# A two-stage kernel (attention to inducing points, then a SwiGLU feed-forward): its 128x128 turns on TensorE are replaced by 32x32 block turns on VectorE

## The chip, the cores and the metric

The kernel runs on one core of a Trainium2 chip. The metric is the device time of one execution in microseconds (us), taken as the median of several runs. A trace of one further execution, taken by the hardware profiler, shows what each engine did: TensorE (PE; its weight loads are listed apart as PEld), VectorE (DVE), ScalarE (ACT), GpSimd (POOL) and SyncE (SP, which here only issues DMAs).

## The reference

Four batches of 12,416 tokens with 128 channels go through attention to 32 inducing points and back, and every token then goes through a feed-forward of width 1,536. All arithmetic is in float32; the three weights arrive as 64-bit floats.

```python
def mab(q, kv):
    s = scale * (q @ kv.transpose(0, 2, 1))
    s = s - s.max(-1, keepdims=True)
    a = np.exp(s); a /= a.sum(-1, keepdims=True) + 1e-09
    return a @ kv
h = mab(I, x)              # per batch: 32 inducing points attend to 12416 tokens
y = mab(x, h)              # the tokens attend to the 32 rows of h
rms = np.sqrt(np.mean(y * y, -1, keepdims=True) + 1e-06)
yn = y / rms * rms_g
g = yn @ w_gate            # 128 -> 1536
out = (g / (1 + np.exp(-g)) * (yn @ w_val)) @ w_out
```

## The kernel before

**The algebra.** A token's y is a mixture of the 32 rows of h. The kernel therefore never forms y for the feed-forward: once per batch it multiplies h (scaled by rms_g) into w_gate and w_val (`stack`, the tiles sg and sv), and feeds the FFN with the token's 32 mixture weights. The weights and the stacks are both split into a high and a low part in the format fp32r, so the contraction is 4 x 32 = 128 rows.

**The FFN.** A unit is 512 tokens (two units of a batch are shorter: 25 units per batch, 100 in all). For each unit, `ffn` runs 12 slots j. A slot is two fp32r matmuls (g, line 504, and v, line 506, into four PSUM banks "gv"), a Silu on ACT (line 508), a product on DVE (u, line 510, which reads v from PSUM) and a float32 matmul with w_out into the accumulator acc (`project`, line 487), which is delayed by two slots with the list `late`. Because four gv banks hold two slots, g of a slot waits for the Silu of two slots before, and v for the product u of two slots before. A finished acc is copied by ACT (oT, line 499), turned on PE by four 128x128 transposes (line 492), copied by DVE (line 494) and stored by one DMA in pieces of 2 KB.

**What is laid between the slots.** `slot(j)` puts other steps behind the g, v, Silu and u of a slot and ahead of its project. Two lists feed it. The attention of the next batch is spread evenly over the slots: turns of x on PE (`turn_x`, line 242, evacuated by DVE and ACT in turn, lines 215 and 217), scores (line 250), one exp of the whole batch on ACT (`exp1`, line 293), turns of the exponentials (line 308) and sums into h (line 320), second scores (line 366) and their turns (line 375), maximum and subtraction on DVE (lines 378 and 379), a second exp (line 383) and the stacks (line 392). The `seam` of the next set of four units runs at fixed slots (`plan`): turn the weights (line 423), form y only for its mean square (a matmul with a block diagonal of h, line 437, a Square on ACT, line 439, a sum on DVE, line 440), take the power -0.5 on POOL (line 447), scale the weights (line 449), turn them back (line 454) and split them into hi and lo (lines 458 and 459). The last step, `split`, has the place (2, 10): third unit of the set, slot 10. At slot 2 of each unit, `gather` copies the next unit's hi and lo rows into the moving tile a with four DMAs.

**The front.** Ahead of the first slot, batch 0's attention runs alone, and the nine pieces of the weights are loaded one by one, converted to float32 by eight DVE operations and one on POOL each, and w_gate and w_val are stored to DRAM for the later batches. Every DMA but two is issued by SP in program order, so a DMA that waits holds up those behind it.

Of the kernel before, what the change touches and what calls it, by code (L numbers as in the profile page):

```python
# [11 lines left out]
I32 = mybir.dt.int32  # L12
# [8 lines left out]
TB = 4  # L21
GB = R * TB


@with_exitstack
def kernel(
# [26 lines left out]

    nc = tc.nc
# [3 lines left out]
    NB = N // P  # L58
    NJ = F // P
    NG = NB // GB  # L60
    H = P // 2
    SCALE = float(1.0 / (C ** 0.5))
    assert C == P and m * R == P and F % 512 == 0 and N % P == 0
    assert NG >= 1 and NB - NG * GB in (0, 1)


    groups = [(g * GB, GB, R, TB) for g in range(NG)]
    if NB > NG * GB:
        groups.append((NG * GB, 1, 1, 1))
    tail = len(groups) > NG  # L70
    TAIL0 = NG * TB * P
    SCW = max(TAIL0 + (P if tail else 0), NB * m)

    sizes = [TB] * (NB // TB) + ([NB % TB] if NB % TB else [])
    if sizes[-1] == 1:
        sizes[-2:] = [TB - 1, 2]
    units = [(sum(sizes[:u]), n) for u, n in enumerate(sizes)]
    NU = len(units)  # L80
    sets = [list(range(s, min(s + R, NU))) for s in range(0, NU, R)]

    def chunks(s):

        at = 0
        for t in range(TB):
            rows = m * sum(units[u][1] > t for u in sets[s])
            if rows:
                yield t, rows, at
            at += rows  # L90

    def rects(s):

        found = []
        for q, u in enumerate(sets[s]):
            n = units[u][1] * P
            if found and found[-1][2] == n:
                found[-1][1] = (q + 1) * m
            else:
                found.append([q * m, (q + 1) * m, n])  # L100
        return found

    def first(s):
        return units[sets[s][0]][0]

    def count(s):
        return sum(units[u][1] for u in sets[s])
# [5 lines left out]
    xnp = pool("xnp", NG)  # L113
    scp = pool("scp", 2)
    stk = pool("stk", 2)
    small = pool("small", 2)
    work = pool("work", 3)
# [4 lines left out]
    up = pool("up", 4)  # L122
# [5 lines left out]
    xT = const.tile([P, NB * P], F32, name="xT")  # L128
    xnat = {}
    xv = x.rearrange("b (p j) c -> b p j c", j=NB)  # L130
    ov = out.rearrange("(b p j) c -> b p j c", b=B, j=NB)

    def load_x(b, g):
        j0, nb, nq, nt = groups[g]
        tag = "xn" if g < NG else "xnt"
        t = xnat[b, g] = xnp.tile([P, nb, C], F32, name=tag, tag=tag, bufs=NG if g < NG else 1)
        nc.sync.dma_start(out=t[:], in_=xv[b, :, j0:j0 + nb, :])

    load_x(0, 0)
# [4 lines left out]
    for g in range(1, len(groups)):  # L144
        load_x(0, g)
# [3 lines left out]
    w32 = [[dram.tile([P, 512], F32, name=f"w{i}{c}") for c in range(F // 512)] for i in range(2)]  # L149
# [4 lines left out]
    mhalf = const.tile([P, GB], F32, name="mhalf")  # L154
# [13 lines left out]
    raws = []  # L168

    def load_w(i, c):  # L170

        src, k = (moe_w_gate, moe_w_val, moe_w_out)[i], 512 // C
        dst = work.tile([P, 512], F32, name="w", tag="sq") if i < 2 else wo.rearrange("p j c -> p (j c)")[:, ts(c, 512)]
        load_w32(i, c, src, dst[:] if i < 2 else dst, k)
        if i < 2:  # L180
            nc.sync.dma_start(out=w32[i][c][:], in_=dst[:])

    def load_w32(i, c, src, dst, k):
        src = src[:, ts(c, 512)] if i < 2 else src[ts(c, k * P), :].rearrange("(j p) c -> p j c", p=P)
        if src.dtype == F32:
            nc.sync.dma_start(out=dst if i < 2 else dst.rearrange("p (j c) -> p j c", c=C), in_=src)
            return
        if not raws:
            t = scp.tile([P, SCW], F32, name="sc")
            raws.extend(t[:, ts(n, 1024)] for n in range(SCW // 1024))  # L190
        words = raws.pop(0).bitcast(I32)
        nc.sync.dma_start(out=words if i < 2 else words.rearrange("p (j c) -> p j c", j=k), in_=src.bitcast(I32))
        raw = words.rearrange("p (f w) -> p f w", w=2)
        low, high = raw[:, :, 0], raw[:, :, 1]
        e, s = (up.tile([P, 512], I32, name="u") for _ in range(2))
        f, r = (silp.tile([P, 512], F32, name="silu") for _ in range(2))
        fi = f.bitcast(I32)
        ve = nc.vector
        ve.tensor_scalar(out=e[:], in0=high, scalar1=20, scalar2=0x7FF, op0=ALU.logical_shift_right, op1=ALU.bitwise_and)
        ve.tensor_scalar(out=e[:], in0=e[:], scalar1=896.0, scalar2=1151.0, op0=ALU.max, op1=ALU.min)  # L200
        ve.tensor_scalar(out=e[:], in0=e[:], scalar1=-896.0, scalar2=float(1 << 23), op0=ALU.add, op1=ALU.mult)
        ve.tensor_scalar(out=s[:], in0=high, scalar1=-(1 << 31), scalar2=0x3F800000, op0=ALU.bitwise_and, op1=ALU.bitwise_or)
        ve.tensor_scalar(out=fi[:], in0=high, scalar1=12, scalar2=9, op0=ALU.logical_shift_left, op1=ALU.logical_shift_right)
        ve.tensor_tensor(out=fi[:], in0=fi[:], in1=s[:], op=ALU.bitwise_or)
        ve.scalar_tensor_tensor(out=r[:], in0=low.bitcast(U32), scalar=2.0 ** -52, in1=s.bitcast(F32)[:],
                                op0=ALU.mult, op1=ALU.mult)
        ve.tensor_tensor(out=f[:], in0=f[:], in1=r[:], op=ALU.add)
        nc.gpsimd.tensor_tensor(out=dst, in0=f[:], in1=e.bitcast(F32)[:], op=ALU.mult)

    turn = [0]  # L210

    def evacuate(dst, src):
        turn[0] += 1
        if turn[0] % 2:
            nc.vector.tensor_copy(out=dst, in_=src)  # L215
        else:
            nc.scalar.copy(out=dst, in_=src)  # L217

    sc, diag, stacks = {}, {}, {}

    def attention(b, load_next):

        st = {}
        steps = []
        add = steps.append

        def open_():
            sc[b] = scp.tile([P, SCW], F32, name="sc")
            st["gmx"] = small.tile([P, len(groups)], F32, name="gmx")

        add(open_)
# [6 lines left out]
        def turn_x(g, q):  # L238
            j0, nb, nq, nt = groups[g]
            ps = bank()  # L240
            for t in range(nt):
                nc.tensor.transpose(ps[:, ts(t, P)], xnat[b, g][:, q * nt + t, :], ident[:])  # L242
            evacuate(xT[:, ds((j0 + q * nt) * P, nt * P)], ps[:, 0:nt * P])

        def scores1(g):
            j0, nb, nq, nt = groups[g]
            n, rows = nt * P, nq * m
            ps = bank()
            for q in range(nq):
                nc.tensor.matmul(ps[ts(q, m), 0:n], indT[:], xT[:, ds((j0 + q * nt) * P, n)], start=True, stop=True)  # L250
            nc.vector.tensor_scalar(
                out=sc[b][0:rows, ds(g * TB * P, n)], in0=ps[0:rows, 0:n], scalar1=1.0, scalar2=None,
                op0=ALU.mult, op1=ALU.max, accum_out=st["gmx"][0:rows, g:g + 1],
            )

        for g, (_, _, nq, _) in enumerate(groups):
            for q in range(nq):
                add(lambda g=g, q=q: turn_x(g, q))
                if g and q == min(1, nq - 1):
                    add(lambda g=g: scores1(g - 1))  # L260
        add(lambda: scores1(len(groups) - 1))

        def max1():
            gmx = st["gmx"]
            mx = small.tile([P, 1], F32, name="mx")
            nc.vector.reduce_max(out=mx[:], in_=gmx[:, 0:NG], axis=AX.X)
            if tail:
                nc.vector.tensor_tensor(out=mx[0:m, :], in0=mx[0:m, :], in1=gmx[0:m, NG:NG + 1], op=ALU.max)
            st["mx"] = mx

        def max2():
            ps = bank()
            nc.tensor.transpose(ps[0:1, 0:P], st["mx"][:], ident[:])
            row = once.tile([1, m], F32, name="row")
            nc.vector.reduce_max(out=row[:], in_=ps[0:1, 0:P].rearrange("p (q m) -> p m q", m=m), axis=AX.X)
            row4 = once.tile([1, R, m], F32, name="row4")
            nc.vector.tensor_scalar_mul(
                out=row4[:], in0=row[:].unsqueeze(1).to_broadcast((1, R, m)), scalar1=-SCALE
            )
            st["row4"] = row4  # L280
# [8 lines left out]
        def exp1():  # L289
            s = sc[b]  # L290
            hl = st["hl"] = once.tile([P, C + 1], F32, name="hl")
            lt = once.tile([P, 1], F32, name="lt")
# [7 lines left out]
        for f in (max1, max2, max3, exp1):  # L300
            add(f)

        def turn_e(g):
            j0, nb, nq, nt = groups[g]
            rows = nq * m
            ps = bank().rearrange("p (t k) -> p t k", k=P)
# [5 lines left out]
        def sum_h(g):  # L312
# [14 lines left out]
            if load_next:  # L327
                load_x(b + 1, g)
# [269 lines left out]
```

## Time and profile before

| | us |
|---|---|
| median of 3 runs (lowest, highest) | 2004.13 (2003.65, 2008.67) |
| the profiled execution, device time | 2005.97 |
| its span in the trace | 2004.2 |
| PE busy, 7445 matmul records | 1910.3 (95%) |
| DVE busy | 1170.0 (58%) |
| ACT busy | 910.5 (45%) |
| POOL busy | 116.7 (6%) |
| first FFN matmul starts at | 149.3 |

The profiled execution lies 1.8 us above the median and its span 1.8 us below its own time. The page gives busy time and shares of each engine, a chain of waits that is followed back from the last instruction, and groups of instructions with their mean duration. In a group a float32 matmul appears as two records. Matmuls overlap in their pipeline, so their spacing in the chain, and not their listed duration, is what one costs. The chain also has a view by windows, and the DMA view gives for a window how many packets each queue moved and which share of 16 DMA engines' time they took.

### The profile page before, as it was taken

What the parts mean: (1) busy time and instruction counts of PE and PEld (TensorE: products, weight loads), DVE (VectorE), ACT (ScalarE), POOL (GpSimd) and SP (SyncE); (2) the same over time, 40 slices, a digit from 0 to 9 for tenths busy, and PEclk for the clock granted to TensorE, in tenths of its full rate; (3) what the DMA queues carried; (4) which work ended last, traced back from release to release, by engine and by line L of the source; (5) the groups of instructions that cost most, each with busy time, mean ns of one, the idle gap of its engine ahead of it and who ended that gap; (6) DMA issues with size and microseconds to landing.
All of it is one profiled execution on the core that took longest, in us unless ns stands there. A gap on an engine that the chain in (4) does not pass through costs nothing.

```text
span 2004.2 us, 22358 instructions
## 1 busy us (share of the span) xinstructions
PE 1910.3 (95%) x7445; PEld 1101.8 (55%) x7445; DVE 1170.0 (58%) x1973; ACT 910.5 (45%) x1550; POOL 116.7 (6%) x92
## 2 busy tenths in 40 slices
PE   4369999999999999999999999999999999999999
PEld 2135555555556555555556655555555655555556
DVE  3655565565756555556666656556575556556555
ACT  1114445445445444544544544544544544444544
POOL 0110000010000000000000000001000000000000
PEclk7589999999999999999999999999999999999999
DMA  5240110410201101130111010000020110111010
GB/s 185 68 167 19 33 30 19 137 44 27 64 27 29 32 22 32 59 123 22 47 38 32 25 32 29 25 28 21 27 64 27 30 32 28 36 32 32 27 33 24
DMA packets 44707, 90.35 MB, mean 45 GB/s; under 512 B 9232, under 2 KB 13360, under 8 KB 41520
## 3 DMA queue, kind: packets, MB, share of 16 engines
q1 hardware_dynamic: 44400, 88.90, 14.3%
q8 instruction: 59, 0.97, 0.2%
q14 instruction: 56, 0.46, 0.1%
q10 hardware_dynamic: 192, 0.02, 0.0%
HBM read 36.45 MB, written 27.00 MB: 32 GB/s over the span
## 4 chain that ended last, share of the span: by engine, by line
PE 91%; DVE 2%; ACT 2%; issue 1%; DMA 0%; POOL 0%; SPq 0%; ACTq 0%; POOLq 0%; DVEq 0%
PE acc L487 50%; PE gv L506 13%; PE gv L504 13%; PE mm L437 4%; PE mm L492 2%; PE mm L242 2%; PE mm L366 1%; PE mm L320 1%; PE mm L250 1%; PE mm L392 1%; PE mm L454 1%; PE mm L423 1%; ACT L508 0%; PE mm L308 0%; PE mm L375 0%
## 5 line engine op out<-in xcount | busy, mean ns | idle before, releaser
L510 DVE TENSOR_TENSOR u<-silu,gv 128x512 f32<-128x512 f32 (+2 forms) x1200 | 804.1, 671 | 707.1 <-ACT silu L508 605.5
L487 PE MATMUL acc<-u,wo 128*128 128x512 f32 (+2 forms) x2400 | 1206.1, 584 | 0.0
L508 ACT ACTIVATE silu<-gv 128x512 f32<-128x512 f32 (+2 forms) x1200 | 701.5, 585 | 836.6 <-PE gv L504 454.0
L504 PE MATMUL gv<-a,sg 128*128 128x512 f32 (+2 forms) x1200 | 930.4, 775 | 20.0 <-ACT silu L508 15.3
L487 PEld LDWEIGHTS acc<-u,wo 128*128 128x128 f32 x2400 | 426.0, 189 | 151.6 <-issue 85.9
L506 PE MATMUL gv<-a,sv 128*128 128x512 f32 (+2 forms) x1200 | 466.2, 389 | 0.0
L504 PEld LDWEIGHTS gv<-a,sg 128*128 128x128 f32 x1200 | 228.0, 190 | 298.2 <-issue 216.8
L506 PEld LDWEIGHTS gv<-a,sv 128*128 128x128 f32 x1200 | 228.7, 191 | 274.2 <-issue 197.6
L447 POOL TENSOR_TENSOR rs<-ms,mhalf 128x16 f32<-128x16 f32 (+2 forms) x28 | 71.8, 2564 | 1567.7 <-DVE ms L444 1567.7
L437 PE MATMUL mm<-diag,aT 128*128 128x512 f32 (+1 forms) x208 | 102.1, 574 | 0.8 <-ACT aT L426 0.8
L440 DVE TENSOR_REDUCE ms<-sq 128x4 f32<-128x512 f32 (+1 forms) x104 | 67.2, 649 | 39.0 <-ACT sq L439 38.7
L439 ACT ACTIVATE sq<-mm 128x512 f32<-128x512 f32 (+1 forms) x104 | 59.2, 569 | 57.3 <-PE mm L437 56.3
L499 ACT COPY oT<-acc 128x512 f32<-128x512 f32 (+2 forms) x100 | 57.3, 573 | 52.1 <-PE acc L487 51.8
L494 DVE COPY o<-mm 128x512 f32<-128x512 f32 (+2 forms) x100 | 66.8, 668 | 1.7 <-PE mm L492 1.7
L492 PE MATMUL mm<-ident,oT 128*128 128x128 f32 x388 | 58.6, 272 | 0.5 <-ACT oT L499 0.5
L492 PEld LDWEIGHTS mm<-ident,oT 128*128 128x128 f32 x388 | 48.2, 140 | 13.3 <-ACT oT L499 0.9
L242 PE MATMUL mm<-ident,xn 128*128 128x128 f32 x288 | 43.1, 272 | 0.0
L437 PEld LDWEIGHTS mm<-diag,aT 128*128 128x128 f32 (+1 forms) x208 | 36.4, 192 | 11.4 <-issue 4.9
L250 PE MATMUL gv<-xT,indT 128*32 128x512 f32 (+1 forms) x50 | 16.8, 889 | 27.0 <-DVE xT L215 25.7
L242 PEld LDWEIGHTS mm<-ident,xn 128*128 128x128 f32 x288 | 35.8, 140 | 9.3
L242 PE MATMUL gv<-ident,xn 128*128 128x128 f32 x96 | 20.4, 382 | 17.6 <-DVE xT L215 14.8
L217 ACT COPY xT<-gv 128x512 f32<-128x512 f32 x12 | 7.0, 586 | 60.2 <-PE gv L242 60.2
(145 smaller groups left out, 699.1 us busy)
## 6 DMA issues: line engine op xcount, KB each, us to landing
xn<-in_x_dram SPq DMA_DIRECT2D x24, 1024.0 KB, 6.2
out_dram<-o SPq DMA_DIRECT2D x92, 256.0 KB, 2.0
a<-hi SPq DMA_DIRECT2D x184, 64.0 KB, 2.0
a<-lo SPq DMA_DIRECT2D x184, 64.0 KB, 2.0
w<-w SPq DMA_DIRECT2D x30, 256.0 KB, 2.8
sc<-in_moe_w_gate_dram SPq DMA_DIRECT2D x3, 512.0 KB, 3.8
sc<-in_moe_w_val_dram SPq DMA_DIRECT2D x3, 512.0 KB, 4.0
sc<-in_moe_w_out_dram SPq DMA_DIRECT2D x3, 512.0 KB, 5.1
```

What stands on the lines that cost most here:

```text
L242: nc.tensor.transpose(ps[:, ts(t, P)], xnat[b, g][:, q * nt + t, :], ident[:])
L437: nc.tensor.matmul(ps[:, 0:k, :], st["aT"][0:rows, ts(t, P)], diag[b][0:rows, 0:k, :], start=True, stop=True)
L439: nc.scalar.activation(sq[:, 0:k, :], ps[:, 0:k, :], AF.Square)
L440: nc.vector.reduce_sum(out=st["ms"][:, ds(at // m, k)], in_=sq[:, 0:k, :], axis=AX.X)
L447: nc.gpsimd.tensor_tensor(out=rs[:, 0:nb], in0=ms[:, 0:nb], in1=mhalf[:, 0:nb], op=ALU.pow)
L487: nc.tensor.matmul(acc[:, 0:T], wo[:, j, :], t[:, 0:T], start=(j == 0), stop=(j == NJ - 1))
L492: nc.tensor.transpose(ps[:, ts(t, P)], oT[:, ts(t, P)], ident[:])
L494: nc.vector.tensor_copy(out=o[:, 0:nt, :].rearrange("p t c -> p (t c)"), in_=ps[:, 0:T])
L504: nc.tensor.matmul(g[:, 0:T], sg[:, ts(j, P)], a[:, 0:T], start=True, stop=True)
L506: nc.tensor.matmul(v[:, 0:T], sv[:, ts(j, P)], a[:, 0:T], start=True, stop=True)
L508: nc.scalar.activation(s[:, 0:T], g[:, 0:T], AF.Silu)
L510: nc.vector.tensor_tensor(out=t[:, 0:T], in0=s[:, 0:T], in1=v[:, 0:T], op=ALU.mult)
```

## The change

**Layout.** Tokens are regrouped into seven sets per batch (five of 16 x 128 tokens, one of 15 x 128 and one of 2 x 128), so that a token's place and a 32-channel strip can be exchanged by turning 32x32 blocks, which VectorE does in one instruction over a whole 128x512 tile (`nc.vector.transpose`, STREAM_TRANSPOSE in the order of instructions below). The units of a batch become 20 of 512 tokens, four of 480 and one of 256.

**What moves to VectorE.** x of batches 1 to 3 is loaded a second time by `load_channels`, in 32-channel strips: four DMAs per set, each of 32 partitions, whose contiguous pieces are 32 channels x 4 bytes = 128 bytes. It is turned in place on DVE. The exponentials (`turn_e`), the second scores (out of PSUM), and the weights in the seam are turned on DVE too. The output is turned by DVE out of the accumulator and stored by four DMAs with pieces of 128 bytes, where before one DMA had pieces of 2 KB. Batch 0 still turns x on PE. The natural x of every set is loaded by four DMAs of 32 partitions.

**The mean square.** It comes from the 32x32 Gram matrix of h: one matmul per set (line 385) in place of four, a turn on DVE, a product on POOL, a sum on DVE. No Square on ACT is left.

**Stacks.** Three column groups of one matmul bank hold the three 512-wide pieces, and twelve DMAs per stack copy the halves to their rows.

**Order.** Subtraction of the maximum moves to POOL (except set 0). The seam has four steps at (1, 2), (1, 6), (1, 9) and (2, 4): split moves from slot 10 to slot 4 of the third unit. `slot` now returns how many projects to issue, and issues none in the three slots ahead of an exp, so that up to five are held back (LAG, `marks`). In the front, raw weights are fetched five at once, only set 0's seam is completed ahead of the FFN, and the second half of the conversions moves into batch 0's second scores. SP's list in the front has the strips of batch 1 twice: once inside `scores2` of batch 0, once in a loop behind the stacks.

```diff
-    def turn_x(g, q):
-            for t in range(nt):
-                nc.tensor.transpose(ps[:, ts(t, P)], xnat[b, g][:, q * nt + t, :], ident[:])
-            evacuate(xT[:, ds((j0 + q * nt) * P, nt * P)], ps[:, 0:nt * P])
+    def load_channels(b, s):
+        w = R * per[s]
+        t = xT[b, s] = xtp.tile([P, w * m], F32, name=f"xT{s}")
+        for k in range(R):
+            nc.sync.dma_start(out=t[ts(k, m), :].rearrange("p (w c) -> p w c", c=m),
+                              in_=of(xrows, b, s)[:, :, ts(k, m)])
...
+        def turn_x(s, k):
+            n = per[s]
+            if b:
+                t = xT[b, s]
+                nc.vector.transpose(out=t[:, ts(k, n * m)], in_=t[:, ts(k, n * m)])
+                return
...
+        def scores2(s):
+            nc.vector.transpose(out=sc[b][:, cols[s]], in_=scores(s, st["hT"][:, 0:m]))
+            if load_next:
+                load_channels(b + 1, s)
...
+        def stack(i):
+            ps = bank()
+            for c, w in enumerate(st.pop(("w", i))):
+                nc.tensor.matmul(ps[ts(c, m), :], st["hg"][:], w[:], start=True, stop=True)
+            hi, lo = (work.tile([P, 512], F32R, name=n, tag="work") for n in ("whi", "wlo"))
...
+            for k, half in enumerate((hi, hi, lo, lo)):
+                for c in range(NC):
+                    nc.sync.dma_start(out=stacks[b][i][ts(k, m), ts(c, 512)].bitcast(F32),
+                                      in_=half[ts(c, m), :].bitcast(F32))
...
-        def square(t, rows, at):
-            ps = ps_m.tile([P, R, C], F32, name="mm", tag="mm")
-            nc.tensor.matmul(ps[:, 0:k, :], st["aT"][0:rows, ts(t, P)], diag[b][0:rows, 0:k, :], start=True, stop=True)
-            nc.scalar.activation(sq[:, 0:k, :], ps[:, 0:k, :], AF.Square)
-            nc.vector.reduce_sum(out=st["ms"][:, ds(at // m, k)], in_=sq[:, 0:k, :], axis=AX.X)
+        def square():
+            ps = ps_m.tile([P, 512], F32, name="mm", tag="mm")
+            nc.tensor.matmul(ps[:, 0:n * m], gram[b][:], st["eT"][:], start=True, stop=True)
+            z = st["z"] = work.tile([P, n, m], F32, name="z", tag="work")
+            nc.vector.transpose(out=z[:].rearrange("p t m -> p (t m)"), in_=ps[:, 0:n * m])
+            nc.gpsimd.tensor_tensor(out=z[:], in0=z[:], in1=weights(b, s), op=ALU.mult)
...
+        def split():
+            aT = work.tile([P, n * m], F32, name="aT", tag="work")
+            nc.vector.transpose(out=aT[:], in_=sc[b][:, cols[s]])
+            hi, lo = split_of[b, s] = [halves.tile([P, 512], F32R, name=k) for k in ("hi", "lo")]
+            nc.vector.tensor_copy(out=hi[:, 0:n * m], in_=aT[:])
+            nc.vector.tensor_tensor(out=lo[:, 0:n * m], in0=aT[:], in1=hi[:, 0:n * m].bitcast(F32), op=ALU.subtract)
...
-        def turn_out(oT):
-            for t in range(nt):
-                nc.tensor.transpose(ps[:, ts(t, P)], oT[:, ts(t, P)], ident[:])
-            nc.vector.tensor_copy(out=o[:, 0:nt, :].rearrange("p t c -> p (t c)"), in_=ps[:, 0:T])
-            nc.sync.dma_start(out=ov[b, :, j0:j0 + nt, :], in_=o[:, 0:nt, :])
+            if j + 1 == NJ:
+                o = outp.tile([P, 512], F32, name="o")
+                nc.vector.transpose(out=o[:, 0:T], in_=acc[:, 0:T])
+                for k in range(R):
+                    nc.sync.dma_start(out=of(out, b, s)[:, ds(q0 * per[s], nb), ts(k, m)],
+                                      in_=o[ts(k, m), 0:T].rearrange("p (w c) -> p w c", c=m))
...
+    gather(0, 0)
+    for i in range(2):
+        f["fetch"](i)
+        f["stack"](i)
+    while queue:
+        convert()
+    if B > 1:
+        for s in range(NS):
+            load_channels(1, s)
...
-            at = [(1, 1), (1, 4), (1, 7), (1, 10), (2, 1), (2, 4), (2, 10)]
+                n, j = ((1, 2), (1, 6), (1, 9), (2, 4))[i]
...
+                if any(k < e <= k + LAG - 2 for e in marks) or len(late) < 2:
+                    return 0
+                return 2 if len(late) > 2 else 1
```

Three places of the order of instructions show what the steps below rest on. The first is TensorE early in batch 0's FFN. Before, a turn of x (xn), of the output (oT) and one of four mean-square matmuls (diag) stand between the slots:

```order
L506 MATMUL gv<-a,sv 128x512
L242 MATMUL mm<-ident,xn 128x128 x4
L487 MATMUL acc<-u,wo 128x512
L504 MATMUL gv<-a,sg 128x512
L506 MATMUL gv<-a,sv 128x512
L492 MATMUL mm<-ident,oT 128x128 x4
L437 MATMUL mm<-diag,aT 128x512
L487 MATMUL acc<-u,wo 128x512
```

In the changed kernel, the same part of the program has one matmul with the Gram matrix, and then only the slots' own:

```order
L431 MATMUL acc<-u,wo 128x512
L441 MATMUL gv<-a,sg 128x512
L443 MATMUL gv<-a,sv 128x512
L385 MATMUL mm<-eT,gram 128x512
L431 MATMUL acc<-u,wo 128x512
L441 MATMUL gv<-a,sg 128x512
```

All turns are gone from TensorE here, and one matmul of 512 columns serves a whole set.

The second place is VectorE where the halves hi and lo of the next set are written. Before, six products u and other work stand between the output copy o and the halves:

```order
L494 COPY o<-mm 128x512
L444 SCALAR_TENSOR_TENSOR ms<-ms,l 128x16
L510 TENSOR_TENSOR u<-silu,gv 128x512 x5
L215 COPY xT<-mm 128x512
L510 TENSOR_TENSOR u<-silu,gv 128x512
L458 CAST hi<-mm 128x512
L459 TENSOR_TENSOR lo<-mm,hi 128x512
```

In the changed kernel only three products stand between them, and both halves wait for DMAs (the DMAHW names are the semaphores of DMAs that still read the old halves for the gather):

```order
L434 STREAM_TRANSPOSE o<-acc 128x512 [waits PE_49]
L447 TENSOR_TENSOR u<-silu,gv 128x512 [waits PE_49,Activation_49] x3
L249 TENSOR_SCALAR sc,gmx<-mm 128x512 [waits PE_49]
L402 STREAM_TRANSPOSE aT<-sc 128x512 [waits Pool_49]
L404 CAST hi<-aT 128x512 [waits DMAHW7_49,DMAHW5_49,DVE_49]
L405 TENSOR_TENSOR lo<-aT,hi 128x512 [waits DMAHW6_49,DMAHW0_49,DVE_49]
L447 TENSOR_TENSOR u<-silu,gv 128x512 [waits PE_49,Activation_49] x3
```

The halves have moved to within two slots of the gather that still reads them, and products u are queued behind them.

The third place is SP's queue at the end of the front. Before, the weights come back from DRAM (w) and the gather of the first units follows:

```order
L387 DMA w<-w_125 128x512
L387 DMA w<-w_128 128x512
L387 DMA w<-w_126 128x512
L387 DMA w<-w_129 128x512
L474 DMA a<-hi 32x512
L474 DMA a<-lo 32x512
```

In the changed kernel, the stacks' copies (whi, wlo) are followed by the strips of batch 1 (xT, the second time), and the gather for the second unit stands behind all of these:

```order
L358 DMA sv<-whi 32x512 x6
L358 DMA sv<-wlo 32x512 x6
L118 DMA xT_882<-in_x_dram 32x64x32 x4
L118 DMA xT_887<-in_x_dram 32x64x32 x4
L118 DMA xT_892<-in_x_dram 32x64x32 x4
L118 DMA xT_897<-in_x_dram 32x64x32 x4
L118 DMA xT_902<-in_x_dram 32x64x32 x4
L118 DMA xT_907<-in_x_dram 32x60x32 x4
L118 DMA xT_912<-in_x_dram 32x8x32 x4
L417 DMA a<-hi 32x512
L417 DMA a<-lo 32x512
```

The gather's place has moved behind 28 strip loads; another 28 of the same strips stand ahead of the first unit's gather.

More of the change, by code (lines that the diff above doesn't have):

```diff
@@ L20 @@
 R = 4
-TB = 4
-GB = R * TB
+LAG = 5
 @with_exitstack
@@ L57 @@
     F = moe_w_gate.shape[1]
-    NB = N // P
     NJ = F // P
-    NG = NB // GB
-    H = P // 2
+    NC = F // 512
     SCALE = float(1.0 / (C ** 0.5))
[L63 to L79, printed above, removed]
-    NU = len(units)
[L81 to L107, printed above, removed]
+    assert C == P and m * R == P and F % 512 == 0 and NC <= R
+    full, rest = divmod(N // P, 16)
+    assert N % P == 0 and full >= 2 and rest < 12
+    per = [16] * full if not rest else [16] * (full - 1) + [15, rest + 1]
+    NS = len(per)
+    start = [P * sum(per[:s]) for s in range(NS)]
+    cols = [slice(m * sum(per[:s]), m * sum(per[:s + 1])) for s in range(NS)]
+    SCW = N // R
+    units = [(s, q, 1) for s in range(full) for q in range(R)] + [(s, 0, R) for s in range(full, NS)]
+    assert all(per[s] * nq <= 16 for s, _, nq in units)
+    NU = len(units)
     def pool(name, bufs, **kw):
@@ L513, in ffn @@
-            slot(j)
-            if len(late) > 1:
-                late.pop(0)()
-            late.append(lambda j=j, t=t: (project(j, t), finish() if j + 1 == NJ else None))
-    weights = [(i, c) for i in range(3) for c in range(F // 512)]
-    for k, f in enumerate(attention(0, B > 1)):
-        f()
-        if k % 4 == 3 and weights:
-            load_w(*weights.pop(0))
-    assert not weights
-    for f in seam(0, 0):
-        f()
-    gather(0, 0)
-    order = [(b, s) for b in range(B) for s in range(len(sets))]
```

516 lines of the change are left out of this document (267 added, 249 removed).

## The prediction

> **What bounds the kernel now.** I read the page's shares first, then the chain that ended last.
>
> ```profile
> PE 1910.3 (95%) x7445; PEld 1101.8 (55%) x7445; DVE 1170.0 (58%) x1973; ACT 910.5 (45%) x1550; POOL 116.7 (6%) x92
> PE 91%; DVE 2%; ACT 2%; issue 1%; DMA 0%; POOL 0%; SPq 0%; ACTq 0%; POOLq 0%; DVEq 0%
> ```
>
> TensorE carries the chain. The chain's rows inside a late unit give the price of a slot and of a turn:
>
> ```profile
> 1706.71 0.23 PE gv L504
> 1706.94 0.23 PE gv L506
> 1707.17 0.86 PE acc L487 x2
> 1708.03 0.23 PE gv L504
> 1708.26 0.24 PE gv L506
> 1708.49 0.44 PE mm L492 x4
> ```
>
> A slot of 512 tokens costs 0.23 + 0.23 + 0.86 = 1.32 us, a unit of twelve 15.8 us, and four 128x128 turns cost 0.44 us between slots, with nothing idle. So whatever is taken off TensorE here is saved in full, unless something else ends last. How much there is, the chain's sum by line from 175 us to the end tells (the row is cut off by the view after L308):
>
> ```profile
> by line: PE acc L487 54.1%; PE gv L506 14.5%; PE gv L504 14.4%; PE mm L437 4.3%; PE mm L492 2.2%; PE mm L242 1.6%; PE mm L366 1.1%; PE mm L320 1.0%; PE mm L250 1.0%; issue 1.0%; PE mm L392 0.8%; PE mm L423 0.6%; PE mm L454 0.6%; PE mm L308
> ```
>
> Of 1829 us, 83% are the FFN, which stays. The stage has one other hole, at each of the six exps (two per later batch); here is the second one of batch 0's FFN:
>
> ```profile
> 493.26 0.25 PE gv L504
> ...
> 495.93 1.80 ACT sc L383
> ...
> 498.74 1.28 ACT L508
> ...
> 500.69 0.50 PE gv L504
> ...
> 502.57 0.43 PE gv L504
> 503.00 0.43 PE gv L506
> 503.42 1.71 PE acc L487 x2
> ```
>
> TensorE waits from 493.5 to 500.7, 7.2 us, for the exp and two table loads. Afterwards the pair of accumulations costs 1.71 in place of 0.86 us, and g and v 0.43: half speed for about 5 us, 2.6 us lost. At the other exp of the batch TensorE waits 7.0 us, and is slow only for the next g and v, 0.5 us lost:
>
> ```profile
> 332.17 0.45 PE mm L492 x4
> ...
> 339.66 0.49 PE gv L504
> 340.15 0.49 PE gv L506
> 340.64 0.44 PE mm L308 x4
> ```
>
> The front is a chain of single steps:
>
> ```profile
> 74.34 1.30 POOL w L208
> 76.15 3.98 DMA sc<-in_moe_w_out_dram
> ...
> 94.74 2.96 ACT sc L293 x2
> ...
> 139.38 2.90 POOL rs L447
> ...
> 147.24 1.98 DMA a<-lo
> ...
> 149.31 0.78 PE gv L504
> ```
>
> Each weight piece is fetched only when the one before is converted and stored, so VectorE waits and x behind it waits too. The first unit starts at 149. The second starts about 171, two slots ahead of the first unit's copy of acc:
>
> ```profile
> L499 ACT COPY oT<-acc x100: 372/586/588, 172.7 to 2000.2; 128x512 f32<-128x512 f32 x92, 128x384 f32<-128x384 f32 x4, 128x256 f32<-128x256 f32 x4
> ```
>
> **TensorE's work.** From the shares of 1829 us go: L437 78.6, L492 40.2, L242 29.3, L423 and L454 11.0 each. L308 and L375 are about 75 turns each at 0.11, 8.2 each. Together 186.5. L392 (14.6) is replaced. Added are 23 full and four small Gram matmuls, 0.86 and 0.11: 20.2; six stacks of three matmuls side by side at 0.86: 5.2; small ones 0.8. Net **175 us less**. That side-by-side column groups run together is what the unchanged sums show (16 products of 128 columns, at four passes as in the 0.86 us for 512, would need 3.4 us one after the other):
>
> ```profile
> 351.15 1.01 PE mm L320 x32
> ```
>
> **The exps.** With five projects held back, TensorE has behind the last unblocked g: three v (0.23 each), two g, and six projects' worth of issue at 0.86, 6.3 us; ACT needs Silu 0.6, table 1.28, exp 3.0, table 1.28, Silu 0.6 and 0.3 of hand-over, 7.1. That leaves 0.8, and the three slots without projects run at the pace of Silu and product instead of TensorE's, which I put at 1.3. So 2.1 in place of 7.1 + 1.6 (mean of the slow stretches after the two kinds of exp): 6.6 saved, six times, **40 us less**.
>
> **VectorE.** The turn itself is in no row. The nearest are copies and reductions of the same 128x512:
>
> ```profile
> L494 DVE COPY o<-mm 128x512 f32<-128x512 f32 x92 | 62.9, 684 | 0.0
> L440 DVE TENSOR_REDUCE ms<-sq 128x4 f32<-128x512 f32 x92 | 62.8, 685 | 38.7 <-ACT sq L439 38.7
> L199 DVE TENSOR_SCALAR u<-sc 128x512 int32<-128x512 int32 x9 | 3.8, 425 | 37.9 <-DMA sc<-in_moe_w_gate_dram 20.1 <-DMA sc<-in_moe_w_val_dram 13.0 <-DMA sc<-in_moe_w_out_dram 4.7
> ```
>
> I take 0.68, bounds 0.43 and twice 0.68. Per batch about 79 turns come (24 of x, 25 of the output, 6 exponentials, 6 scores, 18 in the seam), 54 us. Away go 25 output copies, 26 sums, 12 evacuations of x, six of scores or exponentials, eight of the stacks and six subtractions: 83 at 0.69, less the six new sums. VectorE's total stays near 285 us a batch, in a shorter batch of about 410: 70%, not the bound. What changes is its bursts. The output copy, product and split stand thus in the trace:
>
> ```profile
> 1710.24 0.34 SPq L495 DMA_DIRECT2D out_dram<-o  x1
> 1710.68 0.51 SPq L474 DMA_DIRECT2D a<-hi  x1
> 1711.24 0.59 SPq L474 DMA_DIRECT2D a<-lo  x1
> 1711.88 0.58 SPq L474 DMA_DIRECT2D a<-hi  x1
> 1712.50 0.59 SPq L474 DMA_DIRECT2D a<-lo  x1
> ```
>
> In the changed kernel SP issues four stores and then this gather. With t0 the end of the old unit's last project (slot 1), the turn of the output ends at t0 + 1.2, four stores at 0.34 to 0.58 end at t0 + 2.6 to 3.5, the gather's issues at t0 + 4.9 to 5.8, and 2.0 us later (the landing above) the halves may be overwritten: t0 + 6.3 to 7.2 for the low one. VectorE stands at the split at t0 + 5.1. It waits, and the products u of slots 5 and 6 wait behind it; v of slot 7 needs u of slot 5 and would start at t0 + 6.8, but gets it at 7.7 to 8.6. So TensorE loses 0.9 to 1.8 us per split, 27 times; I take 1.3, 35 us. The stacks' copies hold two of three `work` buffers that the seam's z needs: another 3 us, three times, 9. Together **45 us more**; bounds 0 (the stores issue quickly, or TensorE has slack that I don't see) and 108 (4 us per split).
>
> **The DMAs.** The strips and the output become pieces of 128 bytes, 49,664 per batch each way, 3,104 on each of 16 DMA engines. The trace has 4-byte pieces (gam, on queue q10 from 4 to 8 us) and 512-byte pieces (ind, on q10 from 0.5 to 4 us), and the gather's 2 KB pieces into 32 partitions (q1, 1701.8 to 1705 us):
>
> ```profile
> q10 hardware_dynamic: 98, 0.00, 1.3%
> q10 hardware_dynamic: 48, 0.02, 2.0%
> q1 hardware_dynamic: 144, 0.20, 26.3%
> ```
>
> The first is 1.3% of 16 x 4 us over 98 packets, 8.5 ns; the second 1.12 us over 32 pieces and 16 completions, 31 ns a piece; the third, less 48 completions, 136 ns per 2 KB, 241 GB/s over 16 engines. Between 8.5 and 31 a line gives 14 ns for 128 bytes, an estimate. A batch of strips is then 43 us of all engines, and 7.2 us for a full set. In the FFN a step comes every 240/77 = 3.1 slots, so a set's strips every 8.2 us: 7.2 + 0.9 of output + 0.6 of gather against 8.2. That lag of 0.5 per set is covered by the ten slots (13 us) between a gather and its use. Hence nothing, at 14 ns.
>
> In the front nothing covers it. VectorE's chain: x turned and scored by about 36, exp to 42, two conversions to 46, sums to 54, set 0's scores and exp to 61, then four conversions of 3.6 each, six sets of scores at 1.4 and set 0's seam, to 94; 24 stack copies at 0.58 reach 110. But the DMAs have from 48 on: x of batch 1 (6.36 MB at 241 GB/s, 26), raw weights and stores 8, strips 43, stacks and gather 7: 132, landed 134. Then the second 43 us of strips, ahead of the second unit's gather, to 178. Against 171 that is **7 us more**: the gain of the faster front is spent on strips loaded twice.
>
> [...]
>
> **The sum.** -175 - 40 + 45 + 7 = -163, from 2005.97: 1843. The median of the runs shown is 1.8 below the profiled execution, so 1841 is the forecast.
>
> **Rivals.** *The pieces are dear, and it is slower than before.* If 128 bytes cost the 31 ns of 512, both strip loads of the front grow by 3,104 x 17 ns, 53 each: 105. In the FFN a set needs 15.9 + 2.0 + 0.6 per 8.2 us, 10.3 behind; six sets less 13 of cover are 49, in each of two batches: 98. Total 1841 + 203 = **2044**. The same sum is level with before at about 28 ns. For it: no row shows 128 bytes, and none a store in such pieces. Against: the 4-byte pieces took 8.5 ns. [...] 10%.
>
> *VectorE's waits take the place of TensorE's work.* Each split costs 4 instead of 1.3, and the turns take twice 0.68, which the bursts of output turn and seam pass on with 1 us per set: 1841 + 63 + 27 = **1931**. For it: the wait on the gather is new, and the u queue behind it. Against: VectorE has 30% free. 15%.
>
> *The DMAs are cheap and the waits hidden.* At 8.5 ns the first unit starts at 115 and the second at 144, 34 earlier, and the splits cost nothing: 1841 - 34 - 45 = **1762**. This is also the case in which "FFN begins once one set is ready" comes true. 15%.
>
> *The change doesn't shorten anything*, since something that I have not seen, a queue's issue time for 2,048 pieces say, grows with it just so: 2%.
>
> **How the numbers follow.** The forecast has 58%, within about 1795 to 1900. Faster by over 0.3% (about what a measurement of this kernel can tell from no change, 6 us): 58 + 15 + 15 = 88%. Within it 2%, slower 10%. The range takes the cheap case at its low end, 1762; at 22 ns a piece the same sums give 50 in the front and 36 in the FFN, 1927, and the waits' case 1931, so the high end is 1940. Outside it lie the dear case's 10%, and some 5 at either end of the others.
>
> **What would show it.** In the changed profile: no turn on PE in the FFN and a chain of about 1.32 us slots; the turn near 0.68; the exps' holes at 2 us; the cast hi waiting for a DMA by some 1 us; the first g near 134 and a hole ahead of the second unit up to 178, with the DMA rows full between. If the second unit starts before 150, the price of a piece is wrong; if TensorE is below 90% in mid-FFN with u late, the price of VectorE's bursts; if g waits for a at many units, it is the dear case.

## The result, and the profile after

| | before | after |
|---|---|---|
| median | 2006.26 us (4 runs, 2003.65 to 2008.67) | 1942.09 us (4 runs, 1940.91 to 1944.83) |
| profiled execution | 2005.97 us | 1944.83 us, span 1943.1 |
| after / before | | 0.9682, 95% interval 0.9663 to 0.9701 |

The changed kernel is 64 us faster, where 163 were forecast; 1942 lies just above the range's high end, 1940. (Line numbers from here on are the changed kernel's; rows of the kernel before and of an experiment carry their own.) Its page, the shares of busy time, the queue of the DMAs and the chain that ended last:

```profile
PE 1722.7 (89%) x6258; PEld 959.7 (49%) x6258; DVE 1156.7 (60%) x2010; ACT 751.2 (39%) x1246; POOL 176.9 (9%) x137
...
q1 hardware_dynamic: 442224, 115.91, 30.3%
...
PE 80%; SPq 9%; DMA 5%; ACT 2%; DVE 2%; issue 1%; DVEq 0%; ACTq 0%
```

TensorE carried 91% of the chain before and carries 80% now; 14% are SP's queue and DMAs, which were nowhere. The two stages tell more. First the windows of the kernel before up to its second unit and from there to the end, then the same of the changed kernel (columns: length, busy time of PE, PEld, DVE, ACT, POOL, granted clock, DMA share, GB/s):

```profile
0.00:171.00 171.00, 95.28 (x539) 50.21 (x540) 88.75 (x184) 31.01 (x46) 17.84 (x23) 0.73 0.36 126
171.00:2004.00 1833.00, 1815.06 (x6908) 1051.62 (x6906) 1081.28 (x1790) 879.54 (x1504) 98.81 (x69) 1.00 0.13 38
```

```profile
0.00:213.00 213.00, 66.86 (x471) 36.88 (x472) 85.53 (x164) 25.46 (x37) 35.67 (x35) 0.70 0.78 159
213.00:1943.00 1730.00, 1655.88 (x5788) 922.77 (x5787) 1071.20 (x1846) 725.77 (x1209) 141.24 (x102) 0.98 0.26 50
```

The front up to the second unit grew from 171 to 213 us, where 178 was forecast: 35 us of the miss. The rest fell from 1833 to 1730, where the forecast had 1833 - 175 - 40 + 45 = 1663: the other 67. TensorE's idle time in that stage rose from 18 to 74 us, and the clock fell to 0.98.

**The holes in the FFN.** Two kinds are long. Here is SP's queue around one that comes in the first two batches, when the next strips are loaded, and then VectorE at the same place:

```profile
516.42 12.53 SPq L118 DMA_DIRECT2D xT<-in_x_dram  x8
529.05 3.00 SPq L436 DMA_DIRECT2D out_dram<-o  x4
532.10 0.54 SPq L417 DMA_DIRECT2D a<-hi  x1
...
533.95 0.59 SPq L417 DMA_DIRECT2D a<-lo  x1
```

```profile
524.92 0.67 DVE L402 STREAM_TRANSPOSE aT<-sc 128x480 f32<-128x480 f32 x1
535.43 0.41 DVE L404 CAST hi<-aT 128x480 fp32r<-128x480 f32 x1 [9.83 <-DMA a<-hi]
536.10 0.66 DVE L405 TENSOR_TENSOR lo<-aT,hi 128x480 fp32r<-128x480 f32 x1 [0.26 <-DMA a<-lo]
536.67 0.68 DVE L447 TENSOR_TENSOR u<-silu,gv 128x512 f32<-128x512 f32 x1
```

Eight strip DMAs take SP 12.5 us to issue; the stores and the gather stand behind them; the split's cast may not overwrite hi until that gather has read it, and the product u stands behind the cast. TensorE runs dry for 9.1 us, until that product is there:

```profile
537.41 2.07 PE L431 MATMUL acc<-u,wo 128*128 128x512 f32 x2 [9.11 <-DVE u L447]
```

The other kind comes once in each of the first three batches, at the gather of the short last unit:

```profile
617.59 2.41 SPq L417 DMA_DIRECT2D a<-hi  x4
620.05 2.49 SPq L417 DMA_DIRECT2D a<-lo  x4
622.58 2.49 SPq L417 DMA_DIRECT2D a<-hi  x4
625.11 2.49 SPq L417 DMA_DIRECT2D a<-lo  x4
```

```profile
618.60 0.70 DVE L402 STREAM_TRANSPOSE aT<-sc 128x512 f32<-128x512 f32 x1
626.36 0.43 DVE L404 CAST hi<-aT 128x512 fp32r<-128x512 f32 x1 [7.06 <-DMA a<-hi]
628.99 0.69 DVE L405 TENSOR_TENSOR lo<-aT,hi 128x512 fp32r<-128x512 f32 x1 [2.21 <-DMA a<-lo]
```

A unit over all four quarters needs 16 DMAs, not four: 10 us of issue at 0.59 each. From 620 to 630 TensorE worked 1.3 us.

**The front.** SP's queue, VectorE at the copies of the stacks, and the FFN's first product and the first of its second unit:

```profile
93.82 14.18 SPq L118 DMA_DIRECT2D xT<-in_x_dram  x8
...
149.16 3.71 SPq L358 DMA_DIRECT2D sg<-whi  x6
...
164.32 44.35 SPq L118 DMA_DIRECT2D xT<-in_x_dram  x28
208.76 0.55 SPq L417 DMA_DIRECT2D a<-hi  x1
```

```profile
113.99 0.68 DVE L354 CAST whi<-gv 96x512 fp32r<-96x512 f32 x1
154.42 0.69 DVE L355 TENSOR_TENSOR wlo<-gv,whi 96x512 fp32r<-96x512 f32 x1 [39.75 <-DMA sg<-whi]
```

```profile
157.14 0.76 PE L441 MATMUL gv<-a,sg 128*128 128x512 f32 x1 [49.46 <-DVE a L194]
...
212.69 0.76 PE L441 MATMUL gv<-a,sg 128*128 128x512 f32 x1 [28.60 <-DMA a<-lo]
```

The stacks' copies stand behind the first strips (VectorE waits 39.8 us for a buffer that they hold) and the second unit's gather behind the second strips, 44.35 us. The first product waits for several things at once, and its row names only the one that the profile shows last, a conversion step; that it was the stacks' copies is shown below, by the run without the first strips.

### The profile page after: what moved, and what is told of

Same layout as the page of the kernel before. It is cut to its first block, busy times and chain, and to the rows that moved or that the text cites. A ratio compares the mean times of both kernels' runs of the same rounds, so it can differ in the third digit from the quotient of the medians.

```text
span 1943.1 us, 20398 instructions
## 1 busy us (share of the span) xinstructions
PE 1722.7 (89%) x6258; PEld 959.7 (49%) x6258; DVE 1156.7 (60%) x2010; ACT 751.2 (39%) x1246; POOL 176.9 (9%) x137
## 4 chain that ended last, share of the span: by engine, by line
PE 80%; SPq 9%; DMA 5%; ACT 2%; DVE 2%; issue 1%; DVEq 0%; ACTq 0%
PE acc L431 48%; PE gv L441 13%; PE gv L443 13%; SPq L118 5%; SPq L417 3%; DMA xn<-in_x_dram 2%; PE mm L245 2%; DMA a<-lo 1%; PE mm L285 1%; DVE u L447 1%; PE mm L385 1%; PE gv L233 1%; ACT silu L445 1%; SPq L358 0%; SPq L436 0%
## 5 line engine op out<-in xcount | busy, mean ns | idle before, releaser
L431 PE MATMUL acc<-u,wo 128*128 128x512 f32 (+2 forms) x2400 | 1212.9, 588 | 62.3 <-DVE u L447 62.2
L431 PEld LDWEIGHTS acc<-u,wo 128*128 128x128 f32 x2400 | 443.2, 190 | 217.8 <-DVE u L447 77.9
L388 POOL TENSOR_TENSOR z<-z,sc 128x512 f32<-128x512 f32 (+2 forms) x28 | 31.8, 1136 | 1276.5 <-DVE z L387 1134.6
L434 DVE STREAM_TRANSPOSE o<-acc 128x512 f32<-128x512 f32 (+2 forms) x100 | 69.2, 692 | 1.6 <-PE acc L431 1.1
L225 DVE STREAM_TRANSPOSE xT<-xT 128x512 f32<-128x512 f32 (+2 forms) x84 | 53.2, 633 | 0.0
L331 POOL TENSOR_TENSOR sc<-sc,mx 128x512 f32<-128x512 f32 (+2 forms) x24 | 22.5, 936 | 220.6 <-ACT silu L445 114.2
L385 PE MATMUL mm<-eT,gram 128*128 128x512 f32 (+2 forms) x56 | 26.0, 545 | 0.5 <-DVE eT L376 0.5
L398 POOL TENSOR_TENSOR sc<-sc,rs 128x512 f32<-128x512 f32 (+2 forms) x28 | 26.1, 933 | 2.2
L355 DVE TENSOR_TENSOR wlo<-gv,whi 96x512 fp32r<-96x512 f32 x2 | 1.4, 686 | 39.8 <-DMA sg<-whi 39.8
L233 PEld LDWEIGHTS gv<-ident,xn 128*128 128x128 f32 x97 | 13.4, 169 | 22.9 <-ACT xT L239 20.1
L405 DVE TENSOR_TENSOR lo<-aT,hi 128x512 fp32r<-128x512 f32 (+2 forms) x28 | 17.4, 621 | 11.6 <-DMA a<-lo 11.3
L198 POOL TENSOR_TENSOR a<-a,o 128x512 f32<-128x512 f32 x9 | 11.7, 1303 | 119.0 <-DVE o L196 119.0
```

Source lines behind the costliest of these rows:

```text
L225: nc.vector.transpose(out=t[:, ts(k, n * m)], in_=t[:, ts(k, n * m)])
L233: nc.tensor.transpose(ps[:, ts(t - k * R, P)], xnat[b, s][:, t, :], ident[:])
L385: nc.tensor.matmul(ps[:, 0:n * m], gram[b][:], st["eT"][:], start=True, stop=True)
L431: nc.tensor.matmul(acc[:, 0:T], wo[:, j, :], t[:, 0:T], start=(j == 0), stop=(j == NJ - 1))
L434: nc.vector.transpose(out=o[:, 0:T], in_=acc[:, 0:T])
```

## The experiments

The theory from these traces: the FFN lost its gain to one wait, the split's on the gather; the front lost it to SP's queue. Ratios are to the kernel before; the changed kernel's own is 0.9682.

**Two buffers for the halves**, which takes away what the split waits for.

```
-    halves = pool("halves", 1)
+    halves = pool("halves", 2)
```

> Edit: two buffers for hi and lo instead of one, so that the split's casts no longer wait for the gather that still reads the old halves. Theory A (the FFN's holes are the split waiting for that gather, with the products u queued behind it on VectorE): the wait of hi on the gather, 69.3 us over 24 times, and that of lo, 11.3, go to nearly nothing; TensorE's idle time from the second unit to the end falls from 74 us to about 25 and the half-clock after the holes goes with it: 1942 - 50 - 10, about 1880 us. Theory B (the gathers themselves come late, since SP's queue is full of strips, stores and 0.59 us issues): the same holes come back as g waiting for a, and only the small waits of the ordinary splits, about 13 us, are saved: about 1928 us.

Measured: 1874.23 us, ratio 0.9339 (0.9325 to 0.9353), 68 us less. Its stage from the second unit on, beside the 1730 us above:

```profile
213.00:1874.00 1661.00, 1639.83 (x5785) 918.35 (x5784) 1072.93 (x1846) 725.19 (x1208) 141.36 (x102) 1.00 0.27 52
```

Idle time falls from 74 to 21 us, TensorE's busy time by another 16, and the clock is 1.00 again. That is theory A's case. The gather's lateness itself cost little; the wait that it put on VectorE cost 68 to 69 us.

**The split six slots later**, one buffer as before.

```
-                n, j = ((1, 2), (1, 6), (1, 9), (2, 4))[i]
+                n, j = ((1, 2), (1, 6), (1, 9), (2, 10))[i]
```

> Edit: the split is issued at slot 10 instead of slot 4 of the same unit, 7.9 us later, with one buffer for the halves as before. Theory A (the split waits because the gather of that unit is still under way): the ordinary waits go, 13 us; at the short last unit, whose gather is 16 DMAs and ends some 10 us after the split's place, 7.5 of 9 us go, three times, with their slow stretches; where strips hold up SP's queue the hole stays as a wait of g for a, 18 us in all: 1942 - 13 - 28, about 1900 us. Theory B (VectorE's total load at that place is what counts, not the wait for the gather): no change or slower, 1940 to 1960 us.

Measured: 1873.19 us, 0.9331 (0.9315 to 0.9346), as good as two buffers. The mechanism is theory A's, but its sizes (28 us saved at the short units, 18 left at the strips) were wrong: 7.9 us later nearly every wait is gone. These are this kernel's accumulations and g (idle time in the last column; it was 62.3 us on u in the changed kernel):

```profile
L431 PE MATMUL acc<-u,wo 128*128 128x512 f32 (+2 forms) x2380 | 1190.6, 583 | 0.7 <-DVE u L447 0.7
L441 PE MATMUL gv<-a,sg 128*128 128x512 f32 (+2 forms) x1187 | 913.1, 769 | 12.6 <-DMA a<-lo 10.2 <-ACT silu L445 2.2
```

What is left is 10 us of g waiting for a, most of it some 2 us at each unit that is gathered with 16 DMAs.

**The second strip loading left out.**

```
-    if B > 1:
-        for s in range(NS):
-            load_channels(1, s)
```

> Edit: the second loading of the strips of batch 1 (the loop behind the stacks) is left out; they are already loaded in scores2 of batch 0. Theory A (the front is a sum in which the second strips' 44 us on the DMA queue end last): the second unit starts at about 169 instead of 213 us and the total falls by 44, to about 1898 us. Theory B (something else is late at the second unit as well, the copies of the stacks, the rows of x or the output's turn): the total falls by under 20, above 1922 us.

Measured: 1910.62 us, 0.9522 (0.9505 to 0.9539), 31 us less and not 44. Theory A had the wrong start: the first unit is itself not through before 183, since its own start is held by the first strips. The second unit's first g:

```profile
182.77 0.80 PE L441 MATMUL gv<-a,sg 128*128 128x512 f32 x1
```

212.7 - 182.8 = 29.9 us, nearly all of what the total lost.

**The first strip loading left out**, the other half of the same.

```
-            if load_next:
+            if load_next and b:
                 load_channels(b + 1, s)
```

> Edit: the first loading of the strips of batch 1 (in scores2 of batch 0) is left out, the second one behind the stacks stays. Theory A (the 24 copies of the stacks, and with them the first unit, stand behind the first strips on SP's queue; VectorE's wait of 39.8 us for whi is that): the first product of the FFN starts at about 125 instead of 157 to 165, the second unit waits for the strips until about 178 instead of 213: 35 us less, about 1907 us. Theory B (VectorE's conversions and seam set the first unit): the first unit starts after 150, total above 1925 us.

Measured: 1908.46 us, 0.9509 (0.9485 to 0.9533), 34 us less. The first product and the second unit's:

```profile
123.08 0.77 PE L441 MATMUL gv<-a,sg 128*128 128x512 f32 x1 [15.21 <-DMA sg<-wlo]
...
178.19 0.77 PE L441 MATMUL gv<-a,sg 128*128 128x512 f32 x1 [27.08 <-DMA a<-lo]
```

Both stand where theory A put them: the first unit waited for the strips ahead of the stacks, not for VectorE.

**The rows of batch 0 on SP alone.**

```
-    load_rows(0, 0, [nc.sync, nc.scalar])
+    load_rows(0, 0, [nc.sync])
...
-        load_rows(0, s, [nc.sync, nc.scalar])
+        load_rows(0, s, [nc.sync])
```

> Edit: all row loads of batch 0 are issued on SP; before, every second one stood on ACT, whose own queue was taken up with them until 29.8 us, so that it copied no turned x before 31. Theory A (the front starts late since ACT was held by its DMA issues): x is turned as it lands, exp1 of batch 0 starts at about 42 instead of 51.8, everything behind it moves up by about 10: about 1932 us. Theory B (the 6.36 MB in pieces for 32 partitions arrive at 222 GB/s and end at about 30 whatever the queue, and what comes later is set by the strips' DMA work): under 4 us, 1938 to 1944.

Measured: 1929.93 us, 0.9615 (0.9596 to 0.9634), 12 us less. ACT's queue in the changed kernel, and its first exp with the rows on SP:

```profile
2.60 27.23 ACTq L112 DMA_DIRECT2D xn<-in_x_dram  x12
29.86 1.28 ACT L239 ACT_TABLE_LOAD   x1 [29.86 <-DMA xn<-in_x_dram]
...
51.81 2.88 ACT L273 ACTIVATE sc<-sc,nbias 128x3104 f32<-128x3104 f32 x1 [3.25 <-DVE nbias L269]
```

```profile
39.76 2.88 ACT L273 ACTIVATE sc<-sc,nbias 128x3104 f32<-128x3104 f32 x1 [3.25 <-DVE nbias L269]
```

ACT, which copies turned x out, made its first copy at 31.2, after its queue had been taken up with issuing until 29.8; without that the exp comes 12 us earlier, and the end too.

**No projects held back at the exps.**

```
-                if any(k < e <= k + LAG - 2 for e in marks) or len(late) < 2:
+                if len(late) < 2:
```

> Edit: the five projects held back ahead of each exp are no longer held back (the condition on the marks goes), the buffers stay. Theory A (before, TensorE was really idle only some 2.4 us at an exp, 14.5 us in six, since its own queue of projects ran on beside ACT's chain; the reserve saves little): the idle time at the exps grows from some 0.8 to 2.4 us each, plus a slow stretch of about 1 us, in all 10 to 16 us more: about 1955 us. Theory B (the prediction's step: 6.6 us at each of six exps): 40 us more, 1982 us.

Measured: 1960.44 us, 0.9761 (0.9739 to 0.9782): 18 us more (16 by the ratios), nearer to A (10 to 16) than to B (40). This is TensorE at the exp that the prediction quoted, in the kernel before:

```profile
497.51 1.02 PE L487 MATMUL acc<-u,wo 128*128 128x512 f32 x2
500.69 0.50 PE L504 MATMUL gv<-a,sg 128*128 128x512 f32 x1 [2.15 <-ACT silu L508]
```

It was at work until 498.5, and idle 2.15 us. The "half speed" that the prediction saw behind this exp shows in the granted clock, and only behind three of the six exps (columns as above):

```profile
502.00:506.00 4.00, 4.00 (x9) 2.32 (x8) 2.35 (x4) 1.10 (x3) 0.00 (x0) 0.57 0.63 196
816.00:820.00 4.00, 4.00 (x10) 2.18 (x10) 1.72 (x3) 1.84 (x4) 0.00 (x0) 0.57 0.00 0
1454.00:1458.00 4.00, 4.00 (x8) 2.16 (x7) 2.61 (x5) 1.15 (x3) 0.00 (x0) 0.59 0.58 180
```

What these three windows lack to a clock of 1.00 is 1.7 us each. All six exps of before together are in the row of g (idle time last):

```profile
L504 PE MATMUL gv<-a,sg 128*128 128x512 f32 (+2 forms) x1187 | 919.2, 774 | 14.5 <-ACT silu L508 14.5
```

The windows around one exp, in the changed kernel and without the reserve:

```profile
360.00:370.00 10.00, 9.78 (x31) 5.16 (x30) 7.22 (x15) 5.15 (x9) 4.05 (x2) 1.00 0.15 34
370.00:380.00 10.00, 9.43 (x27) 4.68 (x26) 4.42 (x9) 7.82 (x9) 1.18 (x2) 1.00 0.16 26
380.00:390.00 10.00, 9.46 (x58) 5.24 (x57) 6.26 (x11) 3.58 (x6) 0.00 (x0) 1.00 0.26 62
```

```profile
370.00:380.00 10.00, 6.85 (x16) 3.56 (x15) 4.92 (x9) 7.54 (x8) 0.00 (x0) 0.83 0.28 52
```

The last row is the one without the reserve. There are 1.3 us of idle time with it and 3.15 without, at a mean clock of 0.83. At the second exp of a batch it is 0.17 against 2.97.

**Strips in the FFN, loaded once, with the late split**, and the same **with the rows on SP**: the version that the others point to.

```
         steps = [f["open_"]]
         add = steps.append
+        add(lambda: load_channels(b, 0))
+        steps += [lambda: None] * 4
         for s in range(NS):
             for k in range(R):
                 add(lambda s=s, k=k: f["turn_x"](s, k))
+                if k == 0 and s + 1 < NS:
+                    add(lambda s=s: load_channels(b, s + 1))
```

(Both other loadings go, and the split stands at slot 10.)

> Edit: the split at slot 10 (1873 us alone), and each batch's strips are loaded once, a set at a time in the FFN ahead of their turns, instead of in scores2 of the batch before. Theory A (what is left to gain over the split at slot 10 is the front's strips, 28 us ahead of the second unit and some 35 ahead of the first, and in the FFN the 7 us of a set have 20 us of room): the second unit starts at about 145 instead of 213, total about 1805 us. Theory B (the strips' issue at 1.6 us each on SP holds up stores and gathers wherever it stands, and VectorE waits for strips at its turns): 8 to 10 us per batch come back, 1825 to 1850 us.

> Edit: the one with the strips loaded in the FFN and the split at slot 10, and all row loads of batch 0 on SP. Theory A (without strips the front is a chain of VectorE's work that begins at exp1): 10 us less than with the strips in the FFN alone, about 1795 us. Theory B (the rows of batch 1, 26 us of DMA work, and the copies of the stacks set the first unit): within 3 us of it.

Measured: 1813.40 us, 0.9034 (0.9016 to 0.9053), and 1800.65 us, 0.8968 (0.895 to 0.8986). Both are theory A's cases, 8 and 6 us above its numbers. The second is 141 us faster than the changed kernel; its FFN starts here:

```profile
109.88 0.77 PE L439 MATMUL gv<-a,sg 128*128 128x512 f32 x1 [14.79 <-DMA sg<-wlo]
117.55 0.77 PE L441 MATMUL gv<-a,sv 128*128 128x512 f32 x1 [6.90 <-DMA sv<-wlo]
```

**The conversions' last two steps on VectorE**, on top of that kernel. (In the kernel before, only the product stood on GpSimd; the change had moved the addition there too.)

```
-            nc.gpsimd.tensor_tensor(out=f[:], in0=f[:], in1=r[:], op=ALU.add)
-            nc.gpsimd.tensor_tensor(out=dst, in0=f[:], in1=e.bitcast(F32)[:], op=ALU.mult)
+            ve.tensor_tensor(out=f[:], in0=f[:], in1=r[:], op=ALU.add)
+            ve.tensor_tensor(out=dst, in0=f[:], in1=e.bitcast(F32)[:], op=ALU.mult)
```

> Edit: the one with the strips in the FFN and the rows on SP, and the last two steps of each weight conversion (an addition and a product, 1.3 us each on GpSimd) on VectorE, whose two-operand steps take 0.69. Theory A (two steps of a conversion, at 0.43 us in the kernel before, take 1.0 on average, 1.37 at most, because GpSimd is at work beside them): they come back to 0.43, a conversion costs VectorE 3.5 + 2 x 0.69 = 4.9 us instead of 4.7, and the total stays within 5 us of the 1801 of that kernel. Theory B (they are slow for another reason, such as the DMA traffic of the rows at that time): they stay at 1.0, a conversion costs VectorE 6.1, nine of them 13 us more in the front: about 1812 us.

Measured: 1803.78 us, 0.8993 (0.8967 to 0.9018), no difference that the intervals show, as theory A has it. Six of nine times L191 takes 0.43 us again and L192 always; the other three L191 are slow, and each lies beside a GpSimd operation. Here is one, VectorE and then GpSimd:

```profile
75.27 1.15 DVE L191 TENSOR_SCALAR u<-u 128x512 int32<-128x512 int32 x1
76.45 0.43 DVE L192 TENSOR_SCALAR u<-u 128x512 int32<-128x512 int32 x1
```

```profile
74.98 1.16 POOL L329 TENSOR_TENSOR sc<-sc,mx 128x512 f32<-128x512 f32 x1 [6.54 <-DVE mx L328]
```

## Why the prediction was wrong

The sign and the largest term were right. Four other terms were mis-sized: the exps, VectorE's bursts, the gathers (put at nothing) and the front.

- **TensorE's work, -175: right.** With the split's wait taken away (two buffers), TensorE's busy time from the second unit on is 1639.8 against 1815.1 before: 175.2 less. Stretches at a lower clock lengthen the two alike, by some 5 us. A turn of 128x512 on VectorE took 0.69 to 0.71 us, as the 0.68 said.
- **The exps, -40: mis-sized, and the step failed in the reading.** "TensorE waits from 493.5 to 500.7, 7.2 us" was read from the chain's rows, which stood on ACT; TensorE had its own projects to do beside them until 498.5. The row to read was its idle time: 2.15 us here, 14.5 in all six exps. In the changed kernel the six leave 4.5 us, so 10 us of idle time were won. The slow stretches, put at 1.6 us per exp, were 1.7 behind three of the six, 5 us, and with two buffers the clock at the exps is 1.00. So some 15 us were won, 25 fewer than forecast. That the reserve works is shown: without it the time is 16 to 18 us longer.
- **VectorE's bursts, +45: the mechanism was right, the size was 69.** That is 53 us of idle time and 16 of slower clock, by the two buffers' stage. All of it is the splits', put at 35; the 9 us for the `work` buffers that the stacks hold did not show, for z waited 2.2 us in all, and that for TensorE. Of the 27 splits most cost under 1.3 us. Five cost about 9: two behind strips, three behind the short unit's gather. The step "the gather's issues end at t0 + 4.9 to 5.8" held for four DMAs and a free queue; the 16 DMAs of the short unit were overlooked, and the strips were compared with the DMA engines' time, not with SP's, which the DMAs of strips held for about 1.6 us each (the rival at 2% had named a queue's issue time, without a size). The rival on VectorE's waits, 1931 us, came nearest to the result, for a part of its reason: the wait, at 2.6 us per split and not 4, and not the turns' price. Its 63 us leave 9 out, since 2.7 us at 27 splits are 73, which would give 1941; that this meets the result is luck, for the exps, the gathers and the front make up 78 of the 102 us missed.
- **The gathers of the last units: not in the sum.** With two buffers the idle time is still 21 us: 4.5 at the exps and 17 elsewhere, 13 more than the 3.4 of before; 10 of them lie at and just behind the units gathered with 16 DMAs. Slower clock costs another 5: 1.7 us each at two of these units, and 1.5 where the front's slow stretch reaches past 213. Together 18.
- **The front, +7: it was +42.** The price of a piece was right (below). What failed is "exp to 42" and with it "the DMAs have from 48 on": ACT issued half the rows of x and copied nothing before 31.2, the exp came at 52, and the rows of batch 1 went out from 64: 16 us late. They took 30 us, not 26. "Stacks and gather 7" were 17.7 us of SP's issue (24 copies at 0.62, and the gather). Only the strips were near: the first ones with the weights' stores between them took 53 us, forecast 43 and 8, and the second ones 44, forecast 43. These are 34 of the 35 us. The three experiments on the front gave 12, 31 and 34 us. "FFN begins once one set is ready" did not come true: the first product stood at 157, behind strips that it doesn't need.

The sum of the misses: 25 + 24 + 18 + 35 = 102 us, between the forecast's 1843 and the profiled 1944.83. The dear pieces (2044) are ruled out. That two of the long holes lie at the strips and three at the short unit is read from the trace; no run took one kind away alone.

## What to carry to other kernels

A stall on the chain that ended last is not the idle time of the engine that bounds the kernel: read that engine's own gaps before pricing what a shorter stall is worth. When a buffer is overwritten, list everything queued ahead of its last reader, in the issue time of that queue, at the unit where the queue is longest, and everything queued behind the writer; a second buffer or a place six slots later cost no time here and was worth 68 us. Transfers that are needed late should not be queued ahead of those that start the main stage: moving the strips behind it and off the front was worth 60 us beside the late split.

## What the runs showed of the hardware

- **A piece of 128 bytes cost 13 ns.** While only strips were loaded, from 166 to 208 us, the queue's row is

```profile
q1 hardware_dynamic: 49079, 6.23, 94.6%
```

  94.6% of 16 engines' 42 us over 49,079 packets, nearly all of them such pieces, 12.95 ns, where 14 was estimated. Stores are no dearer: from 1700 to 1760 us 18.5% of 16 x 60 us went to 8,192 pieces of 128 bytes of the output, 512 of 2 KB and 512 completions, which at the 136 and 8.5 ns of before leaves 12.6 ns a piece.
- **Loads of x into 32 partitions ran at half the rate of those into 128.** Here are the windows from 10 to 15 us, while x is loaded, of before and of after:

```profile
10.00:15.00 5.00, 3.89 (x27) 2.41 (x25) 0.00 (x0) 1.26 (x3) 0.00 (x0) 1.00 1.00 423
```

```profile
10.00:15.00 5.00, 4.21 (x19) 3.81 (x20) 0.85 (x2) 0.00 (x0) 0.00 (x0) 1.00 1.02 223
```

  423 against 223 GB/s, at full engines both times, in pieces of 8 KB both times, and with two queues issuing in the second. x landed at 30 us for that reason, at 20 before.
- **Two VectorE steps took longer beside GpSimd's.** L191 and L192 took 0.43 us before and 1.0 on average in the changed kernel, up to 1.39, beside GpSimd's 1.3 us. In the last experiment the L191 shown above ends at 76.42 and GpSimd's operation, which began first, at 76.14; the other two slow L191 also end 0.3 us behind GpSimd's operation. What makes them slow beside it was not shown.
